# Moving the reloads of attention's results and of wo, and later steps for the quotients, in a fused linear-attention and MLP kernel

## The chip, the cores and the metric

The kernel runs on one core of one Trainium2 chip. The metric is device time in microseconds (us) of one execution. The profile is one profiled execution of the same program; its times count from the first instruction (the span's start). Engines are named as the profile names them: PE (TensorE, matmuls), PEld (PE's weight loads), DVE (VectorE), ACT (ScalarE), POOL (GpSimd), SP (SyncE, which here issues nearly all DMAs).

## What is computed

```python
x = A_x                                  # 2048 tokens x 640
xn = _layernorm(x)
return x + A(xn) + B(xn)

# A: 32 heads of 20; per head a learned feature map (two softmaxes) on q and k, then
num = phi_q @ (phi_k^T v);  den = phi_q @ (phi_k^T 1) + 1e-6
A = (num / den) @ wo
# B: pre-layernorm channel MLP, 640 -> 1728 -> 640
B = gelu(_layernorm(xn) @ w1 + b1) @ w2 + b2
```

All is float32. The kernel gets there with float32r matmuls: each operand is split into a high part (written by ACT) and a low part, the rest (written by DVE or POOL), and a product takes three matmuls, high x high, high x low, low x high.

## The kernel before

**Blocks and stages.** The 2048 tokens are four blocks of 512. First comes the MLP of blocks 0 and 1 (to about 216 us), then the projections and feature maps of attention, tile by tile (to about 440 us), and then the stage that matters here: the MLP of blocks 2 and 3 with attention's numerators, denominators and quotients beside it, and at the end the output product with wo for all four blocks.

**PE's order** is written out by hand in that last stage. The hidden units come in 7 groups g of two strips of 128 (the last strip is half full). For g = 1 to 5, `cross` (L411) does the first layer of both blocks in a Strassen-like form, `second(g, 2)` and `second(g, 3)` (L331) the second layer; the latter runs inside the next group's `cross` or, for g = 5, inside group 6. For g = 6, `passes` (L286) does a block's first layer in its first step (five triples of matmuls, then ten matmuls, L304 and L305) and the second layer in five more steps, whose sums into `acc` are L328. The order at the end is: first layer of (6, 2); second(5, 3); first layer of (6, 3); second layer of (6, 2); second layer of (6, 3); output.

**Ticks.** Nearly every triple of matmuls (`mm3`, L70 to L72) is followed by `mlp.tick()`. A tick first runs what was put off with `mlp.after(n, step)` for n ticks, and then takes one step of the generator `mlp.beside`, so that work of ACT, DVE, POOL and SP is written at a chosen distance between PE's matmuls. In this stage the instructions of DVE, ACT and POOL keep their written order (`manual_schedule`), and each of these engines works its instructions in order: one that waits holds all behind it. SP's instructions are not under `manual_schedule`; their order is set by the scheduler when the program is built.

**Attention beside the MLP.** `attend` (L1306) walks through the four blocks. In `groups` a block takes 50 ticks (60 for block 0): for each of eleven groups of features it loads `e`, splits it (ACT L1199, POOL L1200), multiplies it with `kvs` (PE L1206, L1207) and adds the two halves of the bank into `ob` (ACT L1216, DVE L1220). Then the block's `quotients` (L1227) runs on, beside the next block's groups, one step a tick: it stores the denominators to DRAM and reloads them as `dt` (L1232 to L1236), waits some ticks, takes the reciprocal on DVE (L1239), stores it (L1240), waits 6 ticks, loads it spread over partitions into the one tile `rx` (L1244 to L1249), waits some ticks, and then for five chunks shuffles rx on DVE (L1255) and multiplies `ob` by it on POOL (L1257), three ticks apart. Blocks 0 and 1 go to DRAM (`ob_dram`, L1259), since the places of `ob` (acc0, acc1) are needed for blocks 2 and 3. `attend` starts at tick 0; with the waits of before, block b's quotients start at tick 61 + 50 b (from block 0 on), and tick 181 begins second(5, 2), 191 the first layer of (6, 2), 196 second(5, 3), 206 the first layer of (6, 3), 211 and 216 the two second layers, 221 the output.

**Reloads at the end.** `cross` uses the tiles tf0 and tf1. When it has done its last group they are reused for `ob` of blocks 0 and 1, loaded from `ob_dram` (L1378 to L1380), and once these are split, for the MLP sums of the same blocks (`a_dram`, L1282). `load_wo` (L1284) loads the two halves (high and low) of wo into the weight places w2 and w0, 1280 KB each, and their last strips into two smaller tiles (L1290). `split` (L1263) makes block b's high and low parts for the output product (ACT L1276, DVE L1278); for block 0 it is run by `first_split`, two chunks a tick, for the others at fixed steps of the output loop (3, 28 and 53). The output loop multiplies with wo, adds the MLP sum on DVE (L1411) and stores (L1412); its tiles take banks 6 and 7 in turn, the second layer's tiles banks 5, 6 and 7.

Of the kernel before, what the change touches and what calls it, by code (L numbers as in the profile page):

```python
# [46 lines left out]
def f(ap):  # L47
    return ap.bitcast(F32)
# [3 lines left out]
def tile_kernel(ctx: ExitStack, tc: tile.TileContext, x, xT, wkT, wqT, wv, wphi, wo, w1, b1, w2, b2,  # L52
# [461 lines left out]
    mlp = Mlp((0, 1, 2, 3), ((0, 2), (1, 3)))  # L514

    def finish(p):
        for _ in p:
            pass
# [490 lines left out]
    for t, i in [(t, i) for t in range(14) for i in range(4)] + TAIL:  # L1009
        if (t, i) in ((4, 0), (8, 0)):  # L1010
            b = t // 4 + 1
# [33 lines left out]
        if (t, i) == (11, 0):  # L1045
            mlp = Mlp((0, 3, 2, 1), ((1, 2), (0, 3)))
# [16 lines left out]
    def pairs(w1t, w2t):  # L1063

        return [(*(w1t[:, 2 * j + p].rearrange("p (c f) -> p c f", f=P) for p in range(2)), w2t[:, 2 * j], w2t[:, 2 * j + 1])
                for j in range(2)]
# [87 lines left out]
    class Attention:  # L1154
# [72 lines left out]
        def quotients(self):  # L1227

            den, rden = d_dram[self.b]
            ob, parts = self.ob, [(slice(0, 20), "(q c) t -> q c t", 4), (slice(20, 30), "(q c) t -> q c t", 2)]  # L1230
            for i, (r, form, q) in enumerate(parts):
                nc.sync.dma_start(den[r].rearrange(form, q=q), ob[30 + i::128 // q])  # L1232
            dt = ep.tile([P, P], F32, name="dt")
            nc.sync.dma_start(dt, den.rearrange("h (q t) -> (h q) t", q=4))
            for i in range(2):
                nc.sync.dma_start(ob[30 + i::32], o_dram[self.b].rearrange("(q i c) t -> i q c t", i=2, c=KC)[i])  # L1236
            for i in range(10):
                yield
            nc.vector.reciprocal(dt, dt)  # L1239
            nc.sync.dma_start(rden.rearrange("h (q t) -> (h q) t", q=4), dt)  # L1240
            for i in range(6):
                yield

            nc.sync.dma_start(rx[0::32], rden[0:20].rearrange(parts[0][1], q=4))  # L1244
            yield
            for o in (0, 32):
                nc.sync.dma_start(rx[o + 1::64], rden[20:30].rearrange(parts[1][1], q=2))
                yield
                nc.sync.dma_start(rx[o + 2::64], rden[30:32].unsqueeze(1).to_broadcast([2, KC, 512]))  # L1249
                yield  # L1250
            for i in range(6):
                yield
            for c in range(KC + 1):
                if c < KC:
                    nc.vector.stream_shuffle(rx[:, c, :], rx[:, c, :], SPREAD)  # L1255
                if c:
                    nc.gpsimd.tensor_tensor(ob[:, c - 1, :], ob[:, c - 1, :], rx[:, c - 1, :], op=ALU.mult)  # L1257
                    if self.b < 2:
                        nc.sync.dma_start(ob_dram[self.b][:, c - 1], ob[:, c - 1])  # L1259
                for i in range(3):  # L1260
                    yield
# [22 lines left out]
    def load_wo():  # L1284

        for p, wd in enumerate(wo_dram):
            w = wp.tile([P, 4, D], F32R, name=f"w{(2, 0)[p]}")
            nc.sync.dma_start(f(w), wd[:, 0:4, :])
            last = rp.tile([P, D], F32R, name=f"r{1 + p}")
            nc.sync.dma_start(f(last), wd[:, 4, :])  # L1290
            wol.append([w[:, kc, :] for kc in range(4)] + [last])

    def first_split():
        for c in range(KC + 1):
            at[0].split(c, nc.vector)
            if c % 2:
                yield

    def both(*gens):
        for _ in zip_longest(*gens):  # L1300
            yield
# [73 lines left out]
        before = mlp.second(g, 3, w2t, hid[1])  # L1375
    for p in range(2):
        nc.sync.dma_start(f(y[3][p][:, 0:4:2]), y_dram[1][p][:, 0:4:2])
    for b in range(2):  # L1378
        at[b].ob = tfp.tile([P, KC, 512], F32, name=f"tf{b}")
        nc.sync.dma_start(at[b].ob, ob_dram[b])  # L1380
    w2t, parts = mlp.take_pair(6, True, 3)
    ws = pairs(w1t, w2t)
    for b in range(2, 4):
        this = mlp.passes(6, b, ws)
        next(this)
        finish(before)
        before = this
        if b == 2:
            for part in parts:
                part()  # L1390
            load_wo()
            mlp.beside = both(mlp.beside, first_split())
    finish(before)

    pw_ = Banks(6, 7)
    step = 0
# [79 lines left out]
```

## Time and profile before

| | |
|---|---|
| three runs | 721.6, 724.23, 724.64 us; median 724.23 |
| the profiled execution | 725.04 us |
| its span, first to last instruction | 723.1 us |
| granted PE clock over the span | 0.997 |
| busy: PE, DVE, POOL, ACT | 706.7, 513.4, 421.2, 341.5 us |
| chain that ended last | PE 78%, DVE 5%, DMA 4%, POOL 3%, ACT 2% |
| DMA | 106.56 MB, mean 147 GB/s |

PE's time is matmul time as the profile models it: matmuls overlap, so a single one has a duration of 0.39 us but they start 0.23 us apart. A row of a timeline gives start, duration, engine, line, operation, tiles (out<-in), and, in brackets, how long the engine had been idle and what ended that. A row of the chain gives start, duration and what the path to the end went through.

### The profile page before, as it was taken

To read this page: it belongs to the slowest core of one execution; us is meant where nothing else is said; L and a number is where in the kernel's file an instruction comes from. 1 tells how busy PE (TensorE), PEld (TensorE's weight loads), DVE (VectorE), ACT (ScalarE), POOL (GpSimd) and SP (SyncE) were. 2 spreads that over 40 slices of the span, in tenths; PEclk is the share of its full clock that TensorE was granted. 3 is DMA by queue.
4 is the path that set the end of the run, shared out by engine and by line. 5 is a ranking of instruction groups with operands and counts; after the bars stand their busy time and mean duration, and the time that the engine had idled before them with its cause. 6 is when DMAs were issued, how large, how long until landed. Compare 5 with 4: busy or idle time off the path is not lost.

```text
span 723.1 us, 9740 instructions
## 1 busy us (share of the span) xinstructions
PE 706.7 (98%) x3381; PEld 592.8 (82%) x3381; DVE 513.4 (71%) x820; ACT 341.5 (47%) x563; POOL 421.2 (58%) x360
## 2 busy tenths in 40 slices
PE   8989999999999999999999999999999999799998
PEld 6868888878888888888888887888888878678886
DVE  7776755978744888788888887556877756785532
ACT  6434554444334454545445455366667746350200
POOL 3521324567245997897778877477788885531100
PEclk9999999999999999999999999999999999999999
DMA  9913643475621228236203419945364478154121
GB/s 330 287 41 101 202 130 96 153 253 178 211 103 79 87 89 245 67 99 220 64 0 73 115 35 359 233 144 144 113 193 131 160 231 309 52 193 142 73 88 73
DMA packets 65767, 106.56 MB, mean 147 GB/s; under 512 B 7462, under 2 KB 31814, under 8 KB 63838
## 3 DMA queue, kind: packets, MB, share of 16 engines
q1 hardware_dynamic: 65414, 105.93, 46.3%
q8 instruction: 26, 0.43, 0.3%
q14 instruction: 23, 0.19, 0.1%
q10 hardware_dynamic: 304, 0.01, 0.0%
HBM read 71.37 MB, written 34.55 MB: 146 GB/s over the span
## 4 chain that ended last, share of the span: by engine, by line
PE 78%; DVE 5%; DMA 4%; POOL 3%; ACT 2%; issue 2%; SPq 0%; DVEq 0%; ACTq 0%; POOLq 0%
PE bank L898 23%; PE bank L70 16%; PE bank L72 15%; PE bank L71 15%; PE bank L968 2%; PE bank L696 2%; POOL m L933 2%; DMA tf<-ob 1%; PE bank L1207 1%; PE bank L1206 1%; DMA rx<-d 1%; POOL m L944 1%; DMA t<-t 1%; DVE sm L936 1%; ACT w L61 1%
## 5 line engine op out<-in xcount | busy, mean ns | idle before, releaser
L898 PE MATMUL bank<-wkh,y 128*128 128x512 f32 (+1 forms) x480 | 139.5, 364 | 0.0
L70 PE MATMUL bank<-y,w 128*128 128x512 f32 (+1 forms) x294 | 114.4, 389 | 1.0 <-ACT m L283 1.0
L72 PE MATMUL bank<-y,w 128*128 128x512 f32 (+1 forms) x294 | 113.8, 387 | 0.0
L71 PE MATMUL bank<-y,w 128*128 128x512 f32 (+1 forms) x294 | 113.7, 387 | 0.0
L64 POOL TENSOR_TENSOR w<-r,w 128x640 fp32r<-128x640 f32 x32 | 52.8, 1664 | 99.1 <-ACT w L61 68.2
L70 PE MATMUL bank<-m,w 128*128 128x512 f32 x260 | 102.8, 395 | 4.4 <-DVE acc L328 4.1
L72 PE MATMUL bank<-m,w 128*128 128x512 f32 x260 | 101.3, 390 | 0.0
L71 PE MATMUL bank<-m,w 128*128 128x512 f32 x260 | 101.3, 390 | 0.0
L898 PEld LDWEIGHTS bank<-wkh,y 128*128 128x128 f32 x480 | 87.5, 188 | 13.2
L898 PE MATMUL bank<-wkl,y 128*128 128x512 f32 (+1 forms) x240 | 87.4, 364 | 0.0
L70 PEld LDWEIGHTS bank<-y,w 128*128 128x128 f32 x294 | 55.3, 188 | 12.4 <-ACT m L283 1.2
L72 PEld LDWEIGHTS bank<-y,w 128*128 128x128 f32 x294 | 55.2, 188 | 11.5 <-POOL w L390 0.3
L71 PEld LDWEIGHTS bank<-y,w 128*128 128x128 f32 x294 | 55.3, 188 | 11.0
L934 ACT ACTIVATE m<-m,rs_all 128x1280 f32<-128x1280 f32 x32 | 43.7, 1366 | 42.8 <-POOL m L933 42.8
L70 PEld LDWEIGHTS bank<-m,w 128*128 128x128 f32 x260 | 48.9, 188 | 16.7 <-DVE acc L328 6.0
L936 DVE TENSOR_REDUCE sm<-m 128x64 f32<-128x1280 f32 x32 | 47.4, 1481 | 15.6 <-ACT m L934 15.4
L898 PE MATMUL bank<-w,y 128*128 128x512 f32 x240 | 57.4, 391 | 0.0
L72 PEld LDWEIGHTS bank<-m,w 128*128 128x128 f32 x260 | 48.8, 188 | 10.3
L71 PEld LDWEIGHTS bank<-m,w 128*128 128x128 f32 x260 | 48.9, 188 | 9.6
L328 DVE TENSOR_TENSOR acc<-bank,acc 128x512 f32<-128x512 f32 x70 | 47.0, 683 | 12.4 <-PE bank L324 6.2
L933 POOL TENSOR_TENSOR m<-m,mx 128x640 f32<-128x640 f32 (+2 forms) x48 | 44.4, 937 | 19.3 <-DVE mx L922 19.3
L898 PEld LDWEIGHTS bank<-w,y 128*128 128x128 f32 x240 | 44.4, 188 | 8.5
(182 smaller groups left out, 1447.8 us busy)
## 6 DMA issues: line engine op xcount, KB each, us to landing
r<-in_w SPq DMA_DIRECT2D x52, 320.0 KB
e<-e SPq DMA_DIRECT2D x40, 256.0 KB
e<-acc SPq DMA_DIRECT2D x52, 160.0 KB
acc<-in_xT SPq DMA_DIRECT2D x4, 1280.0 KB
t<-t SPq DMA_DIRECT2D x8, 512.0 KB
tf<-t SPq DMA_DIRECT2D x2, 1536.0 KB
xb<-in_x SPq DMA_DIRECT2D x8, 320.0 KB
xq<-in_xT SPq DMA_DIRECT2D x10, 256.0 KB
```

The source lines that it names most:

```text
L61: nc.scalar.activation(hi, src, AF.Copy)
L64: eng.tensor_tensor(lo, src, f(hi), op=ALU.subtract)
L70: nc.tensor.matmul(ps, lh, rh, start=first, stop=False, **kw)
L71: nc.tensor.matmul(ps, lh, rl, start=False, stop=False, **kw)
L72: nc.tensor.matmul(ps, ll, rh, start=False, stop=last, **kw)
L328: nc.vector.tensor_tensor(acc[b][:, m, :], pw, acc[b][:, m, :], op=ALU.add)
L696: nc.tensor.matmul(ps[:, u * nh * DF:(u + 1) * nh * DF], raw[:nh * DH, u * P:(u + 1) * P], wpt[:nh * DH, g, :nh, 1:], start=True, stop=True)
L898: nc.tensor.matmul(ps, lh[:, kc, c], rh[:, kc], start=n == 0, stop=n == 3 * KC - 1)
L933: subs[n, t] = nc.gpsimd.tensor_tensor(ep[:, s], a, b, op=ALU.subtract)
L934: exps[n, t] = nc.scalar.activation(e, e, AF.Exp, scale=rs_all[:, t:t + 1])
L936: nc.vector.tensor_reduce(sm, e.rearrange("p s (h f) -> p (s h) f", f=DH), axis=AX, op=ALU.add)
L968: nc.tensor.matmul(kvp[g // 2][:, (g % 2) * 240:(g % 2) * 240 + 240].rearrange("p (s f) -> p s f", s=4), v[:, g * VS:(g + 1) * VS], ft[:, ...
```

## The change

Four things move; no instruction is added or taken away.

- In `quotients` the wait before the reciprocal becomes 13 ticks instead of 10, and the wait after the loads of rx 12 instead of 6. This holds for all four blocks.
- The reload of block 0's `ob`, written behind second(5, 2), is now written 8 ticks after second(5, 3), in the third tile of the second layer of (6, 2).
- `load_wo` and block 0's splits, written behind second(5, 3), are now written behind the second layer of (6, 2).
- The reload of block 1's `ob` is now written behind the second layer of (6, 3), ahead of the output loop.

```diff
@@ quotients
-            for i in range(10):
+            for i in range(13):
                 yield
             nc.vector.reciprocal(dt, dt)
             nc.sync.dma_start(rden.rearrange("h (q t) -> (h q) t", q=4), dt)
@@ quotients
                 yield
                 nc.sync.dma_start(rx[o + 2::64], rden[30:32].unsqueeze(1).to_broadcast([2, KC, 512]))
                 yield
-            for i in range(6):
+            for i in range(12):
                 yield
             for c in range(KC + 1):
@@ end of the MLP
-    for b in range(2):
+
+    def load_ob(b):
         at[b].ob = tfp.tile([P, KC, 512], F32, name=f"tf{b}")
         nc.sync.dma_start(at[b].ob, ob_dram[b])
+
     w2t, parts = mlp.take_pair(6, True, 3)
     ws = pairs(w1t, w2t)
     for b in range(2, 4):
         this = mlp.passes(6, b, ws)
         next(this)
         finish(before)
         before = this
         if b == 2:
             for part in parts:
                 part()
+            mlp.after(8, lambda: load_ob(0))
+        else:
             load_wo()
             mlp.beside = both(mlp.beside, first_split())
     finish(before)
+    load_ob(1)
```

## The prediction

> **What bounds the kernel now.** I read the busy line of the page first, then PE's busy time in stretches of 5 us, then PE's timeline around each pause, then the chain and the other engines' timelines behind it.
>
> ```profile
> PE 706.7 (98%) x3381; PEld 592.8 (82%) x3381; DVE 513.4 (71%) x820; ACT 341.5 (47%) x563; POOL 421.2 (58%) x360
> ```
> ```profile
> 605.00:610.00 5.00, 5.00 (x24) 4.14 (x23) 3.93 (x5) 3.66 (x8) 4.52 (x3) 1.00 1.01 400
> ...
> 615.00:620.00 5.00, 1.07 (x5) 0.61 (x4) 3.70 (x6) 0.00 (x0) 2.94 (x2) 0.95 0.57 168
> 620.00:625.00 5.00, 5.00 (x17) 3.95 (x17) 3.04 (x8) 2.50 (x4) 1.28 (x1) 0.71 0.00 0
> ...
> 640.00:645.00 5.00, 3.60 (x17) 2.65 (x16) 4.58 (x8) 2.34 (x5) 0.85 (x1) 1.00 0.69 258
> ```
>
> PE is the bound, 98% busy over the span. So time is won or lost only where PE pauses or its clock sinks. The columns are the stretch, its length, busy time of PE, PE's weight loads, DVE, ACT and POOL, then the granted clock, the DMA share and GB/s: PE is full at 605, nearly empty at 615, slow at 620 (clock 0.71, 17 matmuls instead of 24) and short again at 640. With an earlier gap there are three places in the reach of this change. PE's timeline gives their sizes and, in brackets, what ended them:
>
> ```profile
> 580.11 0.39 PE L71 MATMUL bank<-y,w 128*128 128x512 f32 x1
> ...
> 587.31 0.50 PE L1207 MATMUL bank<-e,kvs 128*128 128x512 f32 x1 [1.20 <-POOL e L1200]
> ```
> ```profile
> 615.33 0.39 PE L72 MATMUL bank<-y,w 128*128 128x512 f32 x1
> 619.64 0.80 PE L1206 MATMUL bank<-m,kvs 128*128 128x512 f32 x1 [3.93 <-DVE acc L1220]
> ...
> 623.08 0.39 PE L304 MATMUL bank<-y,w 128*128 128x512 f32 x1
> ...
> 641.46 0.39 PE L324 MATMUL bank<-m,w 128*128 128x512 f32 x1
> 643.25 0.50 PE L70 MATMUL bank<-m,w 128*128 128x512 f32 x1 [1.40 <-DVE acc L328]
> ```
>
> The yardstick is the stretch from 623.08 to 641.46: 81 matmuls in 18.38, 0.227 us each. **Wait 1**: 619.64 - 615.33 is 4.31; less one step, 4.08 us are lost. Then eight steps take 623.08 - 619.64 = 3.44 instead of 1.82, another 1.62, at the low clock. Together 5.70. **Wait 2**: 22 steps from 580.11 to 587.31 take 7.20 instead of 4.99: 2.21 lost. **Wait 3**: 643.25 - 641.46 - 0.227 = 1.56 lost. Together 9.47.
>
> On the low clock behind wait 1 the Trainium skill ("TensorE: Matmul & The Clock Gate", What's actually happening) says that an idle window of about 3.4 us halves the clock, and that it takes such a window of work to come back. The trace agrees: 4.08 us idle were followed by 3.44 us of slow matmuls, the two shorter waits by none.
>
> What causes wait 1 is in the chain, and in DVE's timeline:
>
> ```profile
> 598.61 0.97 DVE dt L1239
> 599.59 0.39 SPq L1240
> 600.03 8.65 DMA tf<-ob
> 608.69 0.51 SPq L1249
> 609.25 0.50 SPq L1247
> 609.79 6.35 DMA rx<-d
> ```
> ```profile
> 616.23 0.01 DVE L1255 LOAD_MASK_SELECT rx<-rx  x1 [4.17 <-DMA rx<-d]
> 616.25 0.72 DVE L1255 STREAM_SHUFFLE rx<-rx 128x512 f32<-128x512 f32 x1
> ```
>
> Block 2's reciprocals, spread by DMA (rx), arrive at 616.2. The first shuffle, L1255, has stood at the head of DVE's queue since 616.23 - 4.17 = 612.06, and behind it the sum L1220, which must free a bank for PE. rx is late because SP issues L1249 only when the reload of block 1's results (tf<-ob, 1280 KB) has landed, and because its 20 KB then take 6.35 us among bulk loads.
>
> **The change part by part.** (a) Later steps of the quotients. A tick comes after three matmuls, 0.68 us, or five, 1.13. The reciprocal moves back 3 ticks, shuffles and products 9, for every block; no instruction is added. By the program's order block 2's quotients start at tick 161, so the first shuffle was at 161 + 10 + 6 + 5 + 6 = 188 and becomes 197, the second tick of second(5,3). Between lie ten matmuls without a tick, L304/305. In the old trace tick 197 is ten steps behind the row at 623.08 (four more of L304/305, then six), 625.4; without wait 1 that is 619.7. With rx there at 616.2 the margin is 3.5 us. The reciprocal costs rx little, since it waited for its own load until 598.61 anyway: at 0.68 a tick 3 ticks are 2.0 us, of which that wait covers most. So wait 1 goes: **-5.70**. What is late next is DVE, which from tick 197 to 210 has five shuffles and four L1220, five L339 and some seven other steps: by the 0.72 above and the 0.67 of the L1220 quoted below some 13 us in 14 of PE's. It just keeps up.
>
> ```profile
> 576.29 1.77 POOL L1257 TENSOR_TENSOR acc<-acc,rx 128x512 f32<-128x512 f32 x1
> ...
> 580.28 1.28 POOL L1257 TENSOR_TENSOR acc<-acc,rx 128x512 f32<-128x512 f32 x1
> ...
> 584.74 1.30 POOL L1257 TENSOR_TENSOR acc<-acc,rx 128x512 f32<-128x512 f32 x1
> 585.99 1.27 POOL L1200 TENSOR_TENSOR e<-e,ph 128x512 fp32r<-128x512 f32 x1
> ```
> ```profile
> 548.30 1.57 POOL L390 TENSOR_TENSOR w<-r,w 128x640 fp32r<-128x640 f32 x1
> ```
>
> The same move meets wait 2. PE waits there for the L1200 that ends at 587.26, and POOL came late to it because block 1's products L1257 (ticks 141 to 153) stand ahead. Moved to 150 to 162, three of them fall behind it: 1.77 + 1.28 + 1.30 = 4.35 us, so it ends near 582.9, while PE, unhindered, wants it at 580.11 + 22 x 0.227 = 585.1. **-2.21.** Block 0's products move too, from ticks 91-103 to 100-112, onto group 4's sums (101-104) and splits (107, 111). The split L390 that group 4's first product needs ended at 549.87; PE wants it at 550.4 (tick 114, counted back from 580.11). One more product ahead of it is 1.3 at the worst, less 0.5 of slack: 0 to 0.8; less than that if POOL, which the earlier products no longer hold, begins the sums sooner. Taken 0.2.
>
> (b) Block 0's splits move from ticks 206-208 to 216-218.
>
> ```profile
> 634.71 2.17 POOL L64 TENSOR_TENSOR w<-r,w 128x640 fp32r<-128x640 f32 x1
> ```
> ```profile
> 635.36 2.07 DVE L1278 TENSOR_TENSOR y<-tf,y 128x512 fp32r<-128x512 f32 x1
> 637.36 0.67 DVE L1220 TENSOR_TENSOR acc<-bank,ts 64x512 f32<-64x512 f32 x1
> 637.96 2.48 DVE L1278 TENSOR_TENSOR y<-tf,y 128x512 fp32r<-128x512 f32 x4
> ```
>
> Their DVE halves, 2.07 (beside POOL's L64) and 4 x 0.62, stood before L308 and so made the second layer's sums L328 late: wait 3, **-1.56**. In the new place they stand among five L328 of some 0.67: 3.1 + 3.4 = 6.5 us of DVE in 25 x 0.227 = 5.7 of PE. Three banks cover the backlog but for the first output tile, which may wait for its own: 0 to 0.8, taken 0.3.
>
> (c) The loads. SP's queue does not keep the written order:
>
> ```profile
> 265.40 0.33 SPq L1040 DMA_DIRECT2D r<-in_wo  x1
> ```
> ```profile
> 299.87 1.12 PE bank L968 x10
> ```
> ```profile
> 604.28 0.34 SPq L1288 DMA_DIRECT2D w<-woh  x1
> ```
> ```profile
> 631.91 0.33 SPq L1288 DMA_DIRECT2D w<-wol  x1
> ```
>
> wo's fourth strip is written in the pass t=6, whose L968 runs at 299.87, yet its load leaves at 265.40, when its buffer is free, 34 us ahead. The two halves of load_wo are one statement in a loop, and leave 27 us apart. The chain's tf<-ob left at 600.03, though it is written behind second(5,2), which PE ends 17 steps before 615.33, at 611.5. A load leaves when its tile is free, not where it is written. So I take the moved reloads to leave about where they did, at no gain and no cost; if they do move, the price is rival B's or D's.
>
> Sum: 725.04 (the profiled execution, 1.94 over its span of 723.1) - 5.70 - 2.21 - 1.56 + 0.2 + 0.3 = 716.1. The median shown is 724.23, 0.8 lower, in runs from 721.6 to 724.64; as what goes is waiting, which differs from run to run, I don't take the 0.8 off again. **Forecast 716.0.**
>
> **Rivals.** B, the reloads do move and PE waits a little. From load_ob(0) (third tile of the second layer) to the output are 40 matmuls, 9.1 us; block 0's results and wo are 4.59 MB, 11.5 us at the 400 GB/s of the row at 605: 2.4 lost, and 1 to 2 more while the output's sums wait for the next 2.6 MB. 719.5 to 720.5. Against it: the issues above.
>
> C, the crowd on POOL moves to block 0 instead of going, 2.2 back: 718.3. For it, the five products and four sums that now fall together; against it, only one L1200 falls among them. C2, rx slides along with its shuffle, since it follows the reciprocal and SP's queue: 5.7 back, 721.8. Against it, the 3.5 us of margin.
>
> D, slower: the reloads leave where they are written and DMA bounds the end. At the 258 GB/s of the row at 640, 4.59 MB take 17.8 us, 8.7 beyond the 9.1 of cover; so long a wait brings the slow clock, 1.6; and the 2.6 MB for block 0's sums and block 1's splits take 10.2 against the 6.8 of two output tiles, 3.4 more. 716.1 + 13.7 = 729.8. It decides once that delay passes the 9 us won. The Trainium skill ("DMA: Bandwidth & Descriptors", Queues, rings and completion order) speaks for it: descriptors are consumed in ring order, so what is issued behind bulk waits for it. The 6.35 us of 20 KB in the chain agree.
>
> **How the numbers follow.** Forecast 0.55 (714 to 718), B 0.17, C 0.09, C2 0.09, D 0.08, others 0.02. A measurement can tell about 0.5%, 3.6 us, from no change. Below 720.6 lie the forecast, C, most of B and a third of C2: faster 0.80. The rest of B and C2: same 0.11. D and half of the others: slower 0.09. The range leaves out D and a little below: 713 to 722; its low end is the forecast less the 3.0 by which the runs before differ.
>
> **What would show it.** Right: no wait of PE on L1220 and none on L1200; clock 1.00 from 600 to the end; L1255 of block 2 with no idle on rx; tf<-ob and w<-woh some 2 us before their old places, not near 640. Wrong: PE waiting for wo at the first output tile, DVE idle at L1239, L1278 or L1255 for a DMA, or POOL late before group 4's first product.

## The result and the profile after

After the change the kernel takes 715.97 us, median of 4 runs (715.64 to 716.96); the kernel before, run beside it, 724.43 (721.6 to 724.78, 4 runs). The ratio on record, over all runs, is 0.9894, 95% interval 0.9867 to 0.9921 (the two medians alone would give 0.9883). The profiled execution of after took 716.96 us (span 715.2, granted clock 0.999), that of before 725.04. Before varies more than after, and its time goes with the granted clock: of 23 further runs of it, the three at a clock of 0.999 or 1.000 took 721.0 to 723.2 us and the eight at 0.995 took 725.6 to 727.4, while after ran at 0.999 to 1.000 each time.

First the busy line of the page of after, then stretches of its windows view with the columns of the prediction: stretch, length, busy time of PE, weight loads, DVE, ACT and POOL, granted clock, DMA share, GB/s.

```profile
PE 704.0 (98%) x3381; PEld 591.2 (83%) x3381; DVE 513.1 (72%) x820; ACT 342.1 (48%) x563; POOL 421.7 (59%) x360
```
```profile
580.00:585.00 5.00, 4.36 (x20) 3.29 (x19) 4.97 (x10) 1.57 (x3) 5.00 (x4) 1.00 0.67 179
...
615.00:620.00 5.00, 5.00 (x23) 4.14 (x23) 2.01 (x5) 3.86 (x6) 1.29 (x1) 1.00 0.69 203
620.00:625.00 5.00, 5.00 (x23) 4.14 (x23) 4.97 (x10) 2.75 (x5) 4.15 (x4) 1.00 0.04 14
...
640.00:645.00 5.00, 5.00 (x23) 3.87 (x22) 5.00 (x9) 0.16 (x1) 0.00 (x0) 1.00 0.28 68
```

The stretches at 615, 620 and 640, which were empty, slow and short, are full, and the clock is 1.00. One pause is left, at 580. PE's timeline of after shows it, and between the first and the last of these rows it shows how long the whole stage took:

```profile
542.21 0.39 PE L1206 MATMUL bank<-m,kvs 128*128 128x512 f32 x1
...
582.83 0.39 PE L72 MATMUL bank<-y,w 128*128 128x512 f32 x1
583.85 0.50 PE L1206 MATMUL bank<-m,kvs 128*128 128x512 f32 x1 [0.64 <-DVE acc L1220]
...
642.94 0.39 PE L324 MATMUL bank<-m,w 128*128 128x512 f32 x1
...
711.47 0.28 PE L72 MATMUL bank<-y,r 128*128 128x256 f32 x1
```

The same two ends in the timeline of before:

```profile
541.57 0.39 PE L1206 MATMUL bank<-m,kvs 128*128 128x512 f32 x1
...
719.39 0.28 PE L72 MATMUL bank<-y,r 128*128 128x256 f32 x1
```

This is the yardstick for all that follows. **Stage time** is the distance from that first L1206 (in block 0's groups) to PE's last matmul: 177.82 us before, 169.26 after, so -8.56. Both ends sit on PE, and between them PE works the same matmuls in the same order; so what the longer steps add up to is the whole difference, but for rounding. What happens ahead of 541 us, which the change doesn't touch, was 0.64 later in the profiled execution of after, and the rest behind the last matmul 0.16 shorter (716.96 - 711.47 = 5.49 against 5.65): -8.56 + 0.64 - 0.16 = -8.08, the difference of the two profiled times.

| lost on PE, us | before | after |
|---|---|---|
| block 0's groups (about 555) | 0 | 0.04 |
| wait 2 (about 580 to 588) | 2.23 | 0.89 |
| wait 1 and its slow matmuls (615 to 623) | 5.68 | 0 |
| wait 3 (about 642) | 1.67 | 0 |
| the output's first tile (643) | 0 | 0.20 |
| sum | 9.58 | 1.13 |

(Each number adds up what the steps of more than 0.26 us exceed 0.23, the normal step to two digits; for wait 3 the slow step behind it is counted too. The sums differ by 8.45; the other 0.1 of the 8.56 is lost in the rounding of some 750 steps.)

### The profile page after: what moved, and what is told of

It reads as the page before. It is cut to its first block, busy times and chain, and to the rows that moved or that the text cites. A ratio compares the mean times of both kernels' runs of the same rounds, so it can differ in the third digit from the quotient of the medians.

```text
span 715.2 us, 9745 instructions
## 1 busy us (share of the span) xinstructions
PE 704.0 (98%) x3381; PEld 591.2 (83%) x3381; DVE 513.1 (72%) x820; ACT 342.1 (48%) x563; POOL 421.7 (59%) x360
## 4 chain that ended last, share of the span: by engine, by line
PE 79%; DVE 7%; POOL 4%; DMA 4%; issue 3%; ACT 2%; SPq 1%; POOLq 0%; DVEq 0%; ACTq 0%
PE bank L898 23%; PE bank L70 16%; PE bank L72 15%; PE bank L71 15%; PE bank L968 2%; PE bank L696 2%; POOL m L933 2%; PE bank L1206 1%; PE bank L1207 1%; POOL w L64 1%; DMA t<-t 1%; DMA xq<-in_xT 1%; POOL m L944 1%; PE bank L323 1%; PE bank L324 1%
## 5 line engine op out<-in xcount | busy, mean ns | idle before, releaser
L328 DVE TENSOR_TENSOR acc<-bank,acc 128x512 f32<-128x512 f32 x70 | 46.9, 684 | 10.5 <-PE bank L72 5.4
L64 DVE TENSOR_TENSOR m<-m,m 128x512 fp32r<-128x512 f32 (+1 forms) x34 | 27.6, 819 | 35.5 <-ACT m L61 35.5
```

Of the source, the lines that this page charges most:

```text
L64: eng.tensor_tensor(lo, src, f(hi), op=ALU.subtract)
L328: nc.vector.tensor_tensor(acc[b][:, m, :], pw, acc[b][:, m, :], op=ALU.add)
```

## The experiments

### Which part of the change does it

**Ticks and the splits' place, with the loads written as before.** The edit, against before, besides the two counts 13 and 12:

```diff
             load_wo()
+        else:
             mlp.beside = both(mlp.beside, first_split())
```

> The kernel before with the new waits of the quotients and block 0's splits behind the second layer of (6, 2), but the reloads of ob and load_wo written where they were. My theory: the written place of a reload decides nothing, so SP issues the same loads in the same order as in the changed kernel and the time is the same, 716 us within 0.7. Rival: without the moved reloads some of the gain is lost, 718 us or more.

715.86 us (715.57 to 716.33, 4 runs), ratio to before 0.9874 (0.9856 to 0.9892); stage time 169.26, the same as after to the hundredth. So the three moves of loads in the change (`load_ob(0)`, `load_wo`, `load_ob(1)`) give and cost nothing. SP's timeline of after shows why:

```profile
597.24 0.65 SPq L1381 DMA_DIRECT2D tf<-ob  x1
...
599.70 0.32 SPq L1381 DMA_DIRECT2D tf<-ob  x1
...
605.75 0.32 SPq L1288 DMA_DIRECT2D w<-woh  x1
...
610.92 0.53 SPq L1244 DMA_DIRECT2D rx<-d  x1
```

The reload of block 1's results, now written behind the last matmul of the MLP (642.94), leaves at 599.70, and wo's high half at 605.75; in before they left at 600.03 and 604.28. The order of SP's 385 DMAs is the same in this kernel and in after, wherever the loads are written. Their times are not: here the first load of rx left at 607.85, in after at 610.92. By so much can rx move between two profiled executions with one order in the queue.

**The ticks alone** (before with 13 and 12):

> The kernel before with only the quotients' waits changed (13 and 12 ticks); reloads, load_wo and block 0's splits stay where they were written. My theory: the later steps carry the gain. Waits 1 and 2 shrink as in the changed kernel (5.7 us, and 2.2 less the 0.8 that is left there), wait 3 stays at about 1.6 us, so about 717.5 us (717 to 719), with tf<-ob issued near 597 and no clock below 1.00 between 600 and 640. Rival: the spread reloads carry it; then this is near 724 us, with PE waiting 4 us at L1206 as before.

720.7 us (718.5 to 721.23, 6 runs), ratio 0.9934 (0.9917 to 0.9952), stage time 173.30: slower than expected. PE's waits in this kernel, from 540 us to the end (line, what it waited for, total us, times, longest):

```profile
PE bank L70 <- DVE acc L328: 2.8, 1, 2.8
PE bank L71 <- DVE m L458: 0.9, 1, 0.9
...
```

Wait 1 is gone, and wait 3 has grown from 1.4 to 2.8. DVE's timeline of the same kernel shows what now stands ahead of the late L328:

```profile
629.07 0.75 DVE L1255 STREAM_SHUFFLE rx<-rx 128x512 f32<-128x512 f32 x1
629.71 1.13 DVE L1278 TENSOR_TENSOR y<-tf,y 128x512 fp32r<-128x512 f32 x1
...
631.37 2.98 DVE L1278 TENSOR_TENSOR y<-tf,y 128x512 fp32r<-128x512 f32 x4
...
634.28 0.72 DVE L1255 STREAM_SHUFFLE rx<-rx 128x512 f32<-128x512 f32 x1
...
637.09 1.27 DVE L328 TENSOR_TENSOR acc<-bank,acc 128x512 f32<-128x512 f32 x2
```

The shuffles, nine ticks later, now fall among block 0's splits. From 629.07 until the two L328 end at 638.36 DVE has no pause; 0.75 + 0.72 of it are shuffles, and the splits, at first beside POOL, take 1.13 and 2.98 (four of them). So the two halves of the change need each other: the later shuffles need the place that the splits leave. What both bring together is not the sum of what each brings.

**The places alone** (after with 10 and 6):

> The changed kernel with the quotients' waits set back to 10 and 6 ticks; only the written places of the reloads, of load_wo and of block 0's splits differ from before. My theory: reloads leave SP where they left before (tf<-ob near 596 and 600), waits 1 and 2 stay (5.7 and 2.2 us), only wait 3 goes: about 723 us (722 to 724). Rival, the spread reloads carry the gain: 716 to 718 us.

724.54 us (721.58 to 726.4, 12 runs), ratio 0.9992 (0.9974 to 1.001): no gain, just outside the expectation. PE's waits from 540 us on:

```profile
PE bank L1206 <- DVE acc L1220: 4.9, 1, 4.9
PE bank L1207 <- POOL e L1200: 1.2, 1, 1.2
```

Wait 3 is gone as foreseen (1.67 to 0.21 with the output's first step), but wait 1 cost 6.69 instead of 5.68: rx arrived at 617.49 instead of 616.23. In the stage 0.39 was won (177.43). Of these 1.3 us, 0.3 is that the whole stage began later in this execution; the rest stays open, and is less than the 3 us by which rx differed above with one order in SP's queue. Whether the splits' place is worth anything by itself was left to a run without wait 1, below.

### What made rx late

**The bulk behind rx.** Before, old ticks, old places; only the two reloads and wo's loads are made to follow block 2's last load of rx in SP's queue:

```diff
-                nc.sync.dma_start(rx[o + 2::64], rden[30:32]...)
+                self.spread = nc.sync.dma_start(rx[o + 2::64], rden[30:32]...).ins
...
-        nc.sync.dma_start(at[b].ob, ob_dram[b])
+        with tc.issue_after(at[2].spread):
+            nc.sync.dma_start(at[b].ob, ob_dram[b])
...
-            load_wo()
+            with tc.issue_after(at[2].spread):
+                load_wo()
```

> The kernel before, with its old waits and places, but the two reloads of ob and load_wo held in SP's queue behind block 2's last load of rx (some 610 us), so that no reload stands ahead of rx. My theory: bulk ahead of rx makes wait 1; without it rx lands some 4 us or more sooner, about the 612 us at which DVE reaches the shuffle, so wait 1 goes (5.7 us), waits 2 and 3 stay (2.2 and 1.6): 719.5 us (718.5 to 721). Rival: rx is late by its own chain of four small DMAs, and the time stays at 724 us.

719.09 us (718.72 to 720.01, 4 runs), ratio 0.9908 (0.9888 to 0.9929). SP's timeline and DVE's, of this kernel:

```profile
598.38 0.32 SPq L1240 DMA_DIRECT2D d<-dt  x1
...
599.92 0.52 SPq L1244 DMA_DIRECT2D rx<-d  x1
...
604.39 0.89 SPq L1381 DMA_DIRECT2D tf<-ob  x2
```
```profile
611.82 0.00 DVE L1255 LOAD_MASK_SELECT rx<-rx  x1
```

The first load of rx in SP's timeline of before:

```profile
605.69 0.52 SPq L1244 DMA_DIRECT2D rx<-d  x1
```

rx leaves 5.8 us earlier than in before (599.92 against 605.69). 1.2 of this is that the store of the reciprocals (L1240), which rx is loaded from, leaves at 598.38 instead of 599.59; 4.6 is the way from that store to the first load, 1.54 us without bulk ahead of it and 6.10 with it. The shuffle finds it there at 611.82 with no idle in front, and wait 1 is gone at the old ticks; waits 2 and 3 stay at 1.20 and 1.40 idle. Stage time 172.50: -5.32 (the 5.68, less 0.37 for two steps of L1206 that stay). So wait 1 needs the bulk ahead of rx's small loads. Which bulk it is, the two reloads or wo's high half (1280 KB each), is not shown, since the edit holds them back together. The change lets the shuffle come when rx is there; this edit brings rx to when the shuffle comes.

**The same with the late place of the splits** (after's places, 10 and 6, bulk behind rx):

> The old ticks (10 and 6), block 0's splits in their late place, and the reloads and wo's loads held behind block 2's last rx load. My theory: with the bulk behind rx wait 1 is gone (the run with old places took 719.1), and the splits' late place then shows its own worth, wait 3's 1.4 to 1.6 us: 717.5, with no wait of L70 on L328 near 638 and wait 2 left. The rival, by which the splits' late place is worth nothing by itself (the run with after's places and the old ticks took 724.5): 719.1.

717.48 us (717.04 to 717.97, 4 runs), ratio 0.9914 (0.9894 to 0.9934). From 540 us on PE waits once, 1.2 us behind POOL's L1200 (wait 2). So the splits' place is worth something by itself once nothing else takes it back: in the stage 172.50 to 171.33, 1.17 us: wait 3's 1.67 goes, and 0.42 comes back at two output tiles (643 and 660 us). The medians, 719.09 and 717.48, don't show it as cleanly: they come from two sets of runs in which before itself took 725.93 and 723.14.

**After, with the bulk behind rx:**

> After as it is, with the reloads and wo's loads held behind block 2's last rx load. My theory: wait 1 is already gone in after, so the order of these loads is worth nothing there: 716.0, within 0.5. The rival, that the bulk still costs something ahead of rx which no wait of TensorE shows: 714 to 715.

716.76 us (715.81 to 717.35, 4 runs), ratio 0.9907 (0.9883 to 0.9931): 0.3 outside the 0.5 that I allowed, but the stage time is 169.25 against 169.26. Two cures for one wait are worth no more than one.

### What truly late reloads cost

In before and after alike the reloads leave near 600. So that rivals B and D can be judged at all, this kernel (after) makes them leave late: they and wo's loads follow block 3's store of its denominators.

```diff
-                nc.sync.dma_start(den[r].rearrange(...), ob[30 + i::128 // q])
+                self.stored = nc.sync.dma_start(den[r].rearrange(...), ob[30 + i::128 // q]).ins
...
-        nc.sync.dma_start(at[b].ob, ob_dram[b])
+        with tc.issue_after(at[3].stored):
+            nc.sync.dma_start(at[b].ob, ob_dram[b])
...
-            load_wo()
+            with tc.issue_after(at[3].stored):
+                load_wo()
```

> The changed kernel, with both reloads of ob and load_wo held behind block 3's store of its denominators in SP's queue (632 us in the changed kernel's trace), so that they leave about as late as they are written. Rival B of the prediction: 4.59 MB at 400 GB/s are 11.5 us, so wo is there near 644 us and PE waits 1 to 3 us at the output: 717 to 719 us. Rival D: at 258 GB/s PE waits 7 us and more and its clock sinks: 724 to 730 us. If when they leave matters nothing: 716 us.

722.63 us (721.36 to 724.8, 10 runs), ratio 0.9968 (0.9951 to 0.9986), 6.7 over after; stage time 175.42, 6.16 over after. It lies between the two ranges expected. SP's timeline, PE's, and the windows view with the columns as above:

```profile
632.93 0.38 SPq L1382 DMA_DIRECT2D tf<-ob  x1
...
636.73 0.45 SPq L1288 DMA_DIRECT2D w<-wol  x1
```
```profile
645.24 0.40 PE L71 MATMUL bank<-y,w 128*128 128x512 f32 x1
647.86 0.50 PE L72 MATMUL bank<-y,w 128*128 128x512 f32 x1 [2.23 <-DMA w<-wol]
...
649.38 0.63 PE L72 MATMUL bank<-y,w 128*128 128x512 f32 x1
```
```profile
645.00:650.00 5.00, 2.77 (x10) 1.95 (x11) 1.89 (x3) 0.00 (x0) 0.00 (x0) 0.93 1.02 420
650.00:655.00 5.00, 5.00 (x18) 3.95 (x17) 1.33 (x3) 2.71 (x5) 0.00 (x0) 0.73 0.74 304
```

With the DMA engines busy all the time (share 1.02, 420 GB/s) PE waits 2.23 for wo's low half; three shorter pauses (0.77, 0.54 and 0.58, two of them behind L328, which stands in DVE's queue behind splits that came late) lie ahead of it, and eight slow matmuls behind it, 0.43 apart, cost 1.54. The 6.7 us are more than the 3.4 to 4.4 that the prediction gave B, and half of D's 13.7. In after neither happened, since the reloads didn't move.

### How much delay

**Only the second wait longer** (10 and 12), **only the first** (13 and 6), otherwise after:

> The changed kernel with 10 ticks before the reciprocal and 12 after the loads of rx. My theory: the shuffles' place counts, and the 12 moves it 6 of the 9 ticks. The first shuffle stands at tick 194, about 614.5 us, and rx lands near 616: 0 to 1.5 us of wait are left, 716 to 717.5 us. Rival: the later reciprocal counts, because DVE stands for dt; then this is near 721 us.

> The changed kernel with 13 ticks before the reciprocal and the old 6 after the loads of rx. My theory: the first shuffle stands at tick 191, about 612.5 us, with rx near 616: most of wait 1 is back (3.5 us, and 1.6 more if the clock sinks), wait 2 about 1: 719.5 to 722 us. Rival, the later reciprocal carries the gain: 716 to 717 us.

Only the second: 717.68 us (717.38 to 718.72, 4 runs), ratio 0.989 (0.987 to 0.991), stage 170.28. Only the first: 718.15 (718.12 to 718.55, 4 runs), ratio 0.9895 (0.9873 to 0.9918), stage 170.62. Both expectations were missed, the first by 0.2 and the second by 1.4, and in both I had put most of what is left at wait 1, which cost next to nothing in either. DVE's timeline of the kernel with only the first wait longer:

```profile
613.52 0.69 DVE L1220 TENSOR_TENSOR acc<-bank,ts 64x512 f32<-64x512 f32 x1
...
617.49 0.01 DVE L1255 LOAD_MASK_SELECT rx<-rx  x1 [2.55 <-DMA r<-in_w]
```

And the sum L1220 that PE waited for in before, in wait 1, from DVE's timeline of before:

```profile
618.89 0.69 DVE L1220 TENSOR_TENSOR acc<-bank,ts 64x512 f32<-64x512 f32 x1
```

With three ticks more the shuffle still finds no rx and DVE stands for 2.55 us. PE loses nothing there: none of its steps between 612 and 620 is longer than 0.26. In before this L1220 stood behind the waiting shuffle; three ticks later the shuffle stands behind it, and it runs at 613.52. So a later shuffle helps in two ways: rx has more time, and what PE needs next is already done when DVE stands. That is read from the order of the rows.

In both kernels the only pause that PE's waits show is wait 2's remainder, 1.67 and 1.86 idle behind L1220, against 0.64 in after. What stands just ahead of that L1220 on DVE shows why: the split L458. DVE's row and POOL's of the kernel with only the second wait longer, then of after:

```profile
581.68 1.94 DVE L458 TENSOR_TENSOR m<-m,m 128x512 fp32r<-128x512 f32 x1
```
```profile
581.51 1.56 POOL L390 TENSOR_TENSOR w<-r,w 128x640 fp32r<-128x640 f32 x1
```
```profile
582.50 0.70 DVE L458 TENSOR_TENSOR m<-m,m 128x512 fp32r<-128x512 f32 x1
```
```profile
582.60 1.74 POOL L1200 TENSOR_TENSOR e<-e,ph 128x512 fp32r<-128x512 f32 x1
```

L458 takes 1.94 us (1.93 in the other kernel) when POOL has begun 0.17 earlier, and 0.70 when DVE has begun first. That is 1.2 us more, and PE's L1206 comes 1.0 and 1.2 us later than in after, counted from the same matmul. The last section comes back to this. No run moved POOL alone, so it is read from the rows.

**Two ticks more than the change** (13 and 14):

> The changed kernel with 14 ticks instead of 12 after the loads of rx. What is left of wait 2 (0.8 us, PE at L1206 behind DVE's L1220, with two shuffles and a split just ahead on DVE) goes if the shuffles stand two ticks later: 715.2 us, no slower than the changed kernel. Rival: two ticks more push block 2's shuffles and block 3's products among the last sums, and a new wait of 1 us or more comes near 630 us: 717 us.

719.22 us (718.77 to 720.56, 4 runs), ratio 0.9911 (0.989 to 0.9932), stage 172.64: neither the expectation nor its rival came, and most of the cost is at neither of the places that I named. PE's waits from 540 us on, then DVE's timeline and SP's, of this kernel:

```profile
PE bank L70 <- DVE acc L339: 1.8, 1, 1.8
...
```
```profile
605.68 0.68 DVE L1220 TENSOR_TENSOR acc<-bank,ts 64x512 f32<-64x512 f32 x1 [3.75 <-DMA ob<-acc]
```
```profile
596.04 0.43 SPq L1381 DMA_DIRECT2D tf<-ob  x1
596.52 0.45 SPq L1259 DMA_DIRECT2D ob<-acc  x1
```

Block 3's first sum (L1220) writes into acc1, which block 1's last chunk must have left (L1259). That store leaves at 596.52, behind the first 1280 KB reload, and lands at 605.68. In after the last store leaves at 596.70 and the reload behind it, at 597.24. It looks like wait 1's mechanism in another place: a small transfer (256 KB) that slips behind a bulk load. That the order of these two alone makes the 3.75 was not tried by itself.

## Why the prediction was right

Forecast 716.0, measured 715.97. By steps:

- **Wait 1 goes, -5.70: right** (5.68 to 0). The margin was there, DVE just kept up (4.97 of 5.00 busy at 620, PE full), and the clock stayed at 1.00. The reason is shown from both sides: rx brought forward wins 5.32 in the stage, the shuffle put back 5.68. Two workings in it don't hold. The 3.5 us of margin took rx where it was, since the later reciprocal would cost it little; in after its first load left at 610.92 instead of 605.69 and its last at 613.12 instead of 609.79, SP having waited 2.7 us on the reload. It still sufficed: no idle time stands before the shuffle at 619.88. And the 21 steps of DVE come to 14.3 us at the prices given, 0.72 and 0.67, not to 13; that 13.12 of the 14.00 from 619.90 were busy is luck, since DVE had fewer of the "other" steps to do.
- **Wait 2 goes, -2.21: the step that was mis-sized.** The mechanism held: POOL no longer ends this wait. But the prediction put all of it down to POOL. DVE's timeline of before and then that of after show what stands ahead of the L1220 that frees the bank:

```profile
576.15 0.75 DVE L458 TENSOR_TENSOR m<-m,m 128x512 fp32r<-128x512 f32 x1
...
578.81 0.75 DVE L1255 STREAM_SHUFFLE rx<-rx 128x512 f32<-128x512 f32 x1
...
580.21 0.73 DVE L1255 STREAM_SHUFFLE rx<-rx 128x512 f32<-128x512 f32 x1
...
582.03 0.67 DVE L1220 TENSOR_TENSOR acc<-bank,ts 64x512 f32<-64x512 f32 x1
```
```profile
576.83 1.15 DVE L458 TENSOR_TENSOR m<-m,m 128x512 fp32r<-128x512 f32 x1
...
579.89 0.75 DVE L1255 STREAM_SHUFFLE rx<-rx 128x512 f32<-128x512 f32 x1
...
581.28 0.74 DVE L1255 STREAM_SHUFFLE rx<-rx 128x512 f32<-128x512 f32 x1
...
583.12 0.67 DVE L1220 TENSOR_TENSOR acc<-bank,ts 64x512 f32<-64x512 f32 x1
```

  The list is the same, two shuffles included, and in before this L1220 already held PE by 0.22 of the 2.23. Counted from the same matmul it ends 0.45 later in after, chiefly because L458 took 1.15 instead of 0.75, and PE, no longer held ahead of it, comes 0.12 earlier: 0.22 + 0.45 + 0.12 = 0.79, and one slow step of 0.1 behind it gives the 0.89 that stayed. "What is late next" was worked out for DVE at block 2's shuffles and left out here.
- **Wait 3 goes, -1.56: right in after, but not by itself.** I took it as independent of (a). With the later ticks and the splits in their old place it grows to 2.8 idle; the splits' place was then worth 4.04 in the stage (173.30 to 169.26), against 1.17 with the old ticks and the bulk behind rx (172.50 to 171.33).
- **Block 0's crowd, +0.2: 0.04.** Its bound of 0.8 was not empty: with the ticks alone PE lost 1.11 + 0.11 there (the wait of 0.9 behind L458 above).
- **Output's first tile, +0.3: 0.20.** Right.
- **The loads don't move, 0: right** to 1.5 us, and it decided the forecast: B and D hang on it.
- **The whole.** In the stage I forecast -8.97 and got -8.56. For the profiled execution I gave 716.1, and it took 716.96, of which 0.48 lie outside the stage. That the median agrees to 0.03 is luck to that extent: the other three runs of after lie 1 us lower than the profiled one.

C and C2 did not happen either: no more than 0.04 was lost in block 0's groups, and rx, whose first load slid by five us and whose last by three, slid less than its shuffle.

Two of the signs named for being right did not come: PE still waits 0.64 on one L1220, and the loads did not leave some 2 us before their old places. They left at 597.24, 599.70 and 605.75 against 596.24, 600.03 and 604.28; block 1's reload left when block 1's last store (L1259) had landed, and that store had moved back with the ticks.

## What to carry to other kernels

When a wait on a transfer is found, look at what was issued ahead of it: a small late-needed load may be cured by moving its consumer, or the bulk behind it; for wait 1 the two were worth nearly the same. A step that is moved meets other work at its new place on each engine that it uses; work out all its instructions for every block, ask what stands behind an instruction that will wait, and expect that two moves which are each worth little may only pay together. Where a scheduler orders the DMA queue, see in the trace where a load leaves before taking its written place for its time.

## What the runs showed of the hardware

**Which engine starts first.** In the kernel with the ticks alone, one DVE split (L458, both inputs in SBUF) starts beside a product on POOL at 553.08 and takes 1.82 us; in after the like split starts at 554.54 beside a product at 554.56 and takes 0.68, and it is POOL that needs longer. DVE's row and POOL's of the kernel with the ticks alone, then of after:

```profile
553.08 1.82 DVE L458 TENSOR_TENSOR m<-m,m 128x512 fp32r<-128x512 f32 x1
```
```profile
553.08 1.28 POOL L1257 TENSOR_TENSOR acc<-acc,rx 128x512 f32<-128x512 f32 x1
```
```profile
554.54 0.68 DVE L458 TENSOR_TENSOR m<-m,m 128x512 fp32r<-128x512 f32 x1
```
```profile
554.56 1.82 POOL L1257 TENSOR_TENSOR acc<-acc,rx 128x512 f32<-128x512 f32 x1
```

Both pairs start within 0.02 us of each other (POOL first by 0.006 us, then DVE first by 0.011, by the trace's nanoseconds), and in each one instruction runs at its usual length and the other is held for about that long: 1.28 + 0.54 = 1.82, and 0.68 + 1.14 = 1.82. PE waited 0.95 us for the held L458 in the kernel with the ticks alone and not at all in after; the same shows in the longer L458 of wait 2's remainder above. The Trainium skill ("SBUF — State Buffer", Who interferes with whom) says that a DVE instruction with two SBUF inputs contends with a GpSimd instruction that reads SBUF, and that the order of issue decides which of the two is blocked, for the whole instruction of the other; these rows agree.

**The clock behind shorter pauses.** In the profiled execution of the kernel with the late reloads the clock fell behind pauses of which none was longer than 2.39 us (0.77, 0.54, 0.58 and 2.39 between 640.28 and 647.86, 4.28 in all), while in that of the kernel with the ticks alone a single pause of 2.93 was followed by one slow step of 0.11. I had counted only on a single long pause. But neither comes every time: three of the ten runs with late reloads kept a clock of 1.000 over the run, and four of the six with the ticks alone had 0.998 and took 720.55 to 721.23 us, against 718.5 and 719.49 for the two at 1.000. So whether pauses add up, and over which stretch of time, stays open.
